# Streaming the columns of a matmul alternately from two halves of its operand

## The chip, the cores and the metric

The kernel runs on one core of one Trainium2 chip. The time is what the device takes for one execution of the program, in microseconds; of several runs the median is given. The profile is that of one further execution, and its own time stands beside the runs below.

## What is computed

Attention in which a query sees only the keys of its own cluster, and then two layers of the form "matmul, activation, matmul" on the 1536 tokens:

```python
scores = np.where(mask, scale * np.matmul(q, k.transpose(0, 1, 3, 2)), -1000000000.0)
attn = softmax(scores)                       # q, k, v: 2 x 8 x 768 x 64
x = heads_side_by_side(np.matmul(attn, v))   # 1536 x 512
h = x @ w_in                                 # 512 -> 2048, layer 1
x = softplus(h) @ w_out                      # 2048 -> 512
h = x @ w_in2                                # the same sizes, layer 2
out = (h * np.clip(h + 3.0, 0.0, 6.0) / 6.0) @ w_out2
```

`mask` is true where the query and the key have the same nearest centroid. The two weights of a layer arrive as float64.

## The kernel before

The attention phase fills the first 268 us or so of the span. It leaves its result transposed in SBUF: `xhi[c]` and `xlo[c]`, four tiles each of 128 features x 1536 tokens. Every float32 operand of the layers is a pair: a rounded part (`hi`, type F32R) and what the rounding left (`lo`). A product is then three matmuls: hi x hi, lo x hi and hi x lo.

The layers run in steps. A step is one layer, one block of 512 tokens (`TB`, three blocks) and one slice f of 128 hidden features (sixteen). For each step:

- `phase_a` (line 172) makes the hidden slice `h` in one PSUM bank, 128 hidden features x 512 tokens: four feature tiles c times three matmuls, twelve in all. The loaded weights are `w[:, c, :]`, a 128x128 piece of w_in; the operand that streams through is `x[c][:, cols]`, 512 tokens in one run.
- `hid_scalar`, `hid_gate`, `hid_hi` and `hid_lo` (lines 865 to 882) read `h` from PSUM and write the activated slice as the pair `ghi`, `glo` in SBUF. In layer 1 ScalarE reads `h` twice (lines 868 and 869) and VectorE makes `glo` (line 882). In layer 2 ScalarE makes `u` from `h` (line 871), VectorE multiplies `u` and `h` (line 875), and ScalarE rounds (line 879).
- `phase_b` (lines 901 and 903) adds the slice's part to four accumulators `y`, one PSUM bank each: again twelve matmuls. In layer 1 (line 901) w_out is loaded and the slice `ghi` or `glo` streams, 512 tokens. In layer 2 (line 903) the slice is loaded and w_out streams, 512 output features, so that the result has tokens as its rows.

After the sixteenth slice of a block `finish_block` reads the four accumulators: in layer 1 into `xhi` and `xlo` (lines 910 and 911), in layer 2 into the tile `o` (lines 918, 919, 924, 926), which SyncE's queue writes to DRAM.

The order is written out by hand. On TensorE `phase_a` of step n is followed by `phase_b` of step n - 2 (`LAG = 2`), so a hidden slice has four groups of twelve matmuls between its making and its use. `h` has four banks, the accumulators one each. The weights are brought from float64 to pairs by ScalarE and VectorE (lines 112 to 147), interleaved with the steps; `convert_abs` (line 112) and `convert_bits` (lines 122 and 126) read one of every two 32-bit words of the loaded weights.

```python
hs[n][:, :TB], w[:, c, :], x[c][:, cols], start=(c == 0 and i == 0), ...
nc.scalar.activation(t["g"], t["h"], AF.Softplus)
nc.tensor.matmul(y[:, :TB], w[:, e, :], x, **fl)
nc.tensor.matmul(y, x[:, e * P:(e + 1) * P], w.rearrange("p c e -> p (c e)"), **fl)
```

Of the kernel before, what the change touches and what calls it, by code (L numbers as in the profile page):

```python
# [12 lines left out]
AF = mybir.ActivationFunctionType  # L13
ALU = mybir.AluOpType
# [8 lines left out]
def cluster_attention_then_two_mlps(  # L23
# [12 lines left out]
    nc = tc.nc  # L36
    P = 128
# [6 lines left out]
    NT, DM = out.shape  # L44
    DFF = w_in1.shape[1]
    NF = DFF // P
    NC = DM // P
# [3 lines left out]
    scale = 1.0 / float(D) ** 0.5  # L51
    assert 2 * D == P and H * C == P and NC == NPAIR and B * S == NT

    def f32(ap):
        return ap.bitcast(F32)
# [20 lines left out]
    xhi = [xpool.tile([P, NT], F32R, name=f"xhi{c}") for c in range(NC)]  # L76
    xlo = [xpool.tile([P, NT], F32R, name=f"xlo{c}") for c in range(NC)]
# [79 lines left out]
    TB = 512  # L157
# [3 lines left out]
    hs = {}  # L161
    last_flip = []

    def phase_a(n, c):
        layer, tb, f = steps[n]
        if c == 0:
            pl, tag = (ps_p, "prep") if n % 4 == 0 else (ps_h[0], "h")
            hs[n] = pl.tile([P, 512], F32, tag=tag, name="h")
        hi_w, lo_w = weights[layer, f, "i"]
        cols = slice(tb * TB, (tb + 1) * TB)  # L170
        for i, (w, x) in enumerate(((hi_w, xhi), (lo_w, xhi), (hi_w, xlo))):
            nc.tensor.matmul(  # L172
                hs[n][:, :TB], w[:, c, :], x[c][:, cols], start=(c == 0 and i == 0), stop=(c == NC - 1 and i == 2)
            )

    def attention():
        with ExitStack() as st, ExitStack() as st_ld, ExitStack() as st_ps:
# [462 lines left out]
            at(87, 6, fetch_w, 0, 6)  # L640
            at(94, 3, open_hidden)
            at(88, 2, phase_a, 0, 0)
            at(90, 1, phase_a, 0, 1)
            at(91, 1, phase_a, 0, 2)
            at(93, 2, phase_a, 0, 3)
            at(94, 3, phase_a, 1, 0)
# [213 lines left out]
    half = const.tile([P, 1], F32, name="half")  # L860
    nc.vector.memset(half, 0.5)

    def hid_scalar(t):

        if t["layer"] == 0:
            nc.scalar.activation(t["g"], t["h"], AF.Softplus)  # L868
            nc.scalar.activation(t["ghi"], t["h"], AF.Softplus)  # L869
        else:  # L870
            nc.scalar.activation(t["u"], t["h"], AF.Relu, bias=half, scale=1.0 / 6.0)  # L871

    def hid_gate(t):
        if t["layer"] == 1:
            nc.vector.scalar_tensor_tensor(t["g"], t["u"], 1.0, t["h"], ALU.min, ALU.mult)  # L875

    def hid_hi(t):
        if t["layer"] == 1:
# [5 lines left out]
    def hidden(layer, h):  # L884
        t = {"h": h, "layer": layer}
        t["ghi"] = tmp.tile([P, TB], F32R, tag="ghi", name="ghi")
        t["glo"] = tmp.tile([P, TB], F32R, tag="glo", name="glo")
        t["g"] = tmp.tile([P, TB], F32, tag="g", name="g")
        if layer == 1:
            t["u"] = tmp.tile([P, TB], F32, tag="u", name="u", bufs=2)  # L890
        return t

    def phase_b(layer, f, g, ys):
        ghi, glo = g["ghi"], g["glo"]
        hi_w, lo_w = weights[layer, f, "o"]
        terms = ((hi_w, ghi), (lo_w, ghi), (hi_w, glo))
        for e, y in enumerate(ys):
            for n, (w, x) in enumerate(terms):
                fl = dict(start=(f == 0 and n == 0), stop=(f == NF - 1 and n == 2))
                if layer == 0:  # L900
                    nc.tensor.matmul(y[:, :TB], w[:, e, :], x, **fl)  # L901
                else:
                    nc.tensor.matmul(y, x[:, e * P:(e + 1) * P], w.rearrange("p c e -> p (c e)"), **fl)  # L903

    def finish_block(layer, tb, ys):
        cols = slice(tb * TB, (tb + 1) * TB)
        if layer == 0:
            for e in range(NC):
                y = ys[e][:, :TB]
                nc.scalar.activation(xhi[e][:, cols], y, AF.Copy)  # L910
                nc.vector.tensor_tensor(xlo[e][:, cols], y, f32(xhi[e][:, cols]), ALU.subtract)
        else:
            for t in range(TB // P):
                o = wpools["val"].tile([P, DM], F32, tag="val", name="o")
                c = tb * (TB // P) + t
                dst = out_v[c // NJ, c % NJ]
                if c == NT // P - 1:
                    nc.scalar.activation(o[:, :DM // 2], ys[t][:, :DM // 2], AF.Copy)
                    nc.vector.tensor_copy(o[:, DM // 2:], ys[t][:, DM // 2:])
                    nc.scalar.dma_start(dst[:, :DM // 2], o[:, :DM // 2])  # L920
                    nc.sync.dma_start(dst[:, DM // 2:], o[:, DM // 2:])
                    continue
                if t % 2:
                    nc.vector.tensor_copy(o, ys[t])
                else:
                    nc.scalar.activation(o, ys[t], AF.Copy)
                nc.sync.dma_start(dst, o)

    LAG = 2
# [8 lines left out]
    with tc.manual_schedule():  # L938
# [11 lines left out]
        for n in range(len(steps) + LAG):  # L950
# [3 lines left out]
            t = None  # L954
            if n < len(steps):
# [3 lines left out]
                t = gs[steps[n]] = hidden(steps[n][0], hs.pop(n)[:, :TB])  # L959
# [9 lines left out]
            if t:  # L969

                with tc.issue_after(last_flip[0].ins):
                    hid_scalar(t)
            do(convert_rest, ci, engine=nc.vector)
            do(convert_abs, ni)
            if t:
                hid_gate(t)
# [6 lines left out]
            if n >= LAG:  # L983
                l, tb, f = s = steps[n - LAG]
                if f == 0:
                    ysd[l, tb] = [
                        ps_y.tile([P, 512], F32, tag=f"y{e}", name=f"y{e}") for e in range(NC)
                    ]
                phase_b(l, f, gs.pop(s), ysd[l, tb])
                if l == 0 and tb == NB - 1:  # L990
                    fetch_w(1, f)
                if f == NF - 1:
                    finish_block(l, tb, ysd.pop((l, tb)))
# [40 lines left out]
```

## Time and profile before

| | us |
|---|---|
| median of three runs | 775.82 |
| the three runs | 774.63, 775.82, 777.75 |
| the profiled execution, its own time | 779.6 |
| its span, first to last instruction | 777.8 |

| engine | busy us | share of the span |
|---|---|---|
| TensorE, matmuls | 761.5 | 98% |
| TensorE, weight loads | 645.0 | 83% |
| VectorE | 457.1 | 59% |
| ScalarE | 409.9 | 53% |
| GpSimd | 150.3 | 19% |

The times of the profile are those of one execution. A matmul's row runs from its start to its modelled end, and the next matmul starts before that end, so rows overlap: how fast matmuls follow each other is read from their starts. "PE" is TensorE's matmuls, "PEld" its weight loads, "DVE" VectorE, "ACT" ScalarE, "POOL" GpSimd, "SP" SyncE. A line number is that of the kernel before.

### The profile page before, as it was taken

How to read it: one execution, taken by the hardware profiler on the slowest of the kernel's cores; microseconds unless marked ns; L12 is line 12 of the kernel's file. 1: busy time of each engine (PE TensorE's matmuls, PEld its weight loads, DVE VectorE, ACT ScalarE, POOL GpSimd, SP SyncE). 2: the span in 40 equal slices, each digit the busy share in tenths (PEclk: the TensorE clock that was granted, in tenths of full speed). 3: DMA queues.
4: the chain of work that ended last, by engine and by line, in shares of the span. 5: the costliest groups of instructions: out<-in, count | busy, mean ns of one | idle time of the engine just before them, and what ended most of it. 6: DMA issues, size and time to landing. Idle time of an engine off the chain costs nothing.

```text
span 777.8 us, 10594 instructions
## 1 busy us (share of the span) xinstructions
PE 761.5 (98%) x3841; PEld 645.0 (83%) x3841; DVE 457.1 (59%) x788; ACT 409.9 (53%) x815; POOL 150.3 (19%) x223
## 2 busy tenths in 40 slices
PE   7989999999999999999999999999999999999998
PEld 6778898899888788888888888888888888888886
DVE  6969889889888999821111276779842322232221
ACT  6869889888998766531121344555532322222222
POOL 3467668767444000000000000000000000000000
PEclk9999999999999999999999999999999999999999
DMA  6645676666463670000000355640000100010001
GB/s 190 178 125 144 172 200 168 157 188 159 113 190 133 223 285 1 1 1 0 1 1 27 109 191 188 201 151 0 1 1 0 55 1 0 1 55 0 1 1 54
DMA packets 40548, 71.32 MB, mean 92 GB/s; under 512 B 4752, under 2 KB 25648, under 8 KB 40496
## 3 DMA queue, kind: packets, MB, share of 16 engines
q1 hardware_dynamic: 40352, 70.52, 30.8%
q8 instruction: 30, 0.49, 0.2%
q14 instruction: 22, 0.18, 0.1%
q10 hardware_dynamic: 144, 0.13, 0.0%
HBM read 46.30 MB, written 3.19 MB: 64 GB/s over the span
## 4 chain that ended last, share of the span: by engine, by line
PE 88%; DVE 3%; ACT 3%; DMA 2%; POOL 2%; issue 1%; POOLq 0%; SPq 0%; ACTq 0%; DVEq 0%
PE h L172 32%; PE y L903 17%; PE y L901 16%; PE t L441 7%; PE pv L456 7%; PE s L411 6%; PE psm L311 2%; DMA q<-in_q 1%; DMA row<-rT 1%; ACT pth L445 1%; DVE nm L419 1%; ACT pr L427 1%; DVE ptl L446 1%; DMA rsb<-row 1%; PE warm L248 0%
## 5 line engine op out<-in xcount | busy, mean ns | idle before, releaser
L172 PE MATMUL h<-xhi,pi 128*128 128x512 f32 x768 | 237.2, 390 | 0.9 <-DVE pi L147 0.8
L172 PEld LDWEIGHTS h<-xhi,pi 128*128 128x128 f32 x768 | 143.7, 188 | 31.0 <-DVE pi L147 1.2
L882 DVE TENSOR_TENSOR glo<-g,ghi 128x512 fp32r<-128x512 f32 x96 | 66.3, 691 | 144.5 <-ACT ghi L869 115.7
L172 PE MATMUL h<-xlo,pi 128*128 128x512 f32 x384 | 149.5, 389 | 0.0
L901 PE MATMUL y<-ghi,po 128*128 128x512 f32 x384 | 118.2, 389 | 0.0
L903 PE MATMUL y<-po,ghi 128*128 128x512 f32 x384 | 118.2, 389 | 0.0
L446 DVE TENSOR_TENSOR ptl<-t,pth 128x384 fp32r<-128x384 f32 x192 | 97.6, 549 | 24.0 <-ACT pth L445 23.0
L875 DVE SCALAR_TENSOR_TENSOR g<-u,h 128x512 f32<-128x512 f32 x48 | 33.0, 687 | 125.1 <-ACT u L871 125.1
L871 ACT ACTIVATE u<-h,half 128x512 f32<-128x512 f32 x48 | 33.0, 687 | 126.1 <-PE h L172 125.8
L411 PE MATMUL s<-K,Q 128*128 128x256 f32 (+1 forms) x384 | 90.2, 356 | 5.6 <-ACT pr L427 3.7
L445 ACT ACTIVATE pth<-t 128x384 fp32r<-128x384 f32 x192 | 85.8, 491 | 15.3 <-PE t L441 14.5
L419 DVE TENSOR_REDUCE nm<-s 128x1 f32<-128x768 f32 x96 | 90.6, 944 | 3.1 <-PE s L411 3.1
L427 ACT ACTIVATE pr<-s,nm 128x768 f32<-128x768 f32 x96 | 86.9, 905 | 3.2 <-DVE nm L419 3.0
L441 PE MATMUL t<-ident,pr 128*128 128x128 f32 x576 | 85.9, 279 | 2.1 <-DVE ptl L446 1.8
L868 ACT ACTIVATE g<-h 128x512 f32<-128x512 f32 x48 | 28.5, 594 | 109.4 <-PE h L172 109.3
L903 PEld LDWEIGHTS y<-po,ghi 128*128 128x128 f32 x384 | 72.1, 188 | 15.0
L172 PEld LDWEIGHTS h<-xlo,pi 128*128 128x128 f32 x384 | 72.1, 188 | 15.0
L901 PEld LDWEIGHTS y<-ghi,po 128*128 128x128 f32 x384 | 72.1, 188 | 15.0
L441 PEld LDWEIGHTS t<-ident,pr 128*128 128x128 f32 x576 | 66.1, 141 | 15.7 <-DVE ptl L446 11.9
L411 PEld LDWEIGHTS s<-K,Q 128*128 128x128 f32 x384 | 66.0, 189 | 15.7 <-ACT pr L427 5.0
L901 PE MATMUL y<-glo,po 128*128 128x512 f32 x192 | 74.7, 389 | 0.0
L903 PE MATMUL y<-po,glo 128*128 128x512 f32 x192 | 74.7, 389 | 0.0
(127 smaller groups left out, 932.5 us busy)
## 6 DMA issues: line engine op xcount, KB each, us to landing
ri<-in_moe_w_in SPq DMA_DIRECT2D x29, 512.0 KB, 4.8
ro<-in_moe_w_out SPq DMA_DIRECT2D x29, 512.0 KB, 8.3
K<-hik SPq DMA_DIRECT2D x31, 192.0 KB, 5.0
Q<-hiq SPq DMA_DIRECT2D x15, 384.0 KB, 3.9
Q<-loq SPq DMA_DIRECT2D x16, 192.0 KB, 5.6
v<-in_v SPq DMA_DIRECT2D x8, 384.0 KB
rsb<-row SPq DMA_DIRECT2D x16, 192.0 KB, 4.1
K<-lok SPq DMA_DIRECT2D x15, 192.0 KB, 4.4
```

The lines of the kernel that those rows point to most:

```text
L172: nc.tensor.matmul(hs[n][:, :TB], w[:, c, :], x[c][:, cols], start=(c == 0 and i == 0), stop=(c == NC - 1 and i == 2))
L411: nc.tensor.matmul(ps[:, n0:n1], Q[i][:, u, j * P:(j + 1) * P], K[i][:, u, n0:n1], start=(u == 0), stop=(u == 1),)
L419: nc.vector.tensor_reduce(nm, st_s[t][:, :S], AX.X, ALU.max, negate=True)
L427: nc.scalar.activation(pr, st_s.pop(t)[:, :S], AF.Exp, bias=st_p[t], accum_out=sums_of[n][:, i, j:j + 1])
L441: nc.tensor.transpose(pt[:, c * P:(c + 1) * P], pr[:, kt * P:(kt + 1) * P], ident)
L445: last_flip[:] = [nc.scalar.activation(dh, src, AF.Copy)]
L446: nc.vector.tensor_tensor(dl, src, f32(dh), ALU.subtract)
L456: nc.tensor.matmul(st_v[h][:, :HALF], vs[:, kt, i, :], st_t[h][u][:, kt, :], start=(kt == 0 and u == 0), stop=(kt == NJ - 1 and u == 1),)
L871: nc.scalar.activation(t["u"], t["h"], AF.Relu, bias=half, scale=1.0 / 6.0)
L882: nc.vector.tensor_tensor(t["glo"], t["g"], f32(t["ghi"]), ALU.subtract)
L901: nc.tensor.matmul(y[:, :TB], w[:, e, :], x, **fl)
L903: nc.tensor.matmul(y, x[:, e * P:(e + 1) * P], w.rearrange("p c e -> p (c e)"), **fl)
```

## The change

Two views of an operand are introduced. `turned` takes 512 columns in the order 0, 256, 1, 257, 2, 258 and so on. The streaming operand of every matmul in both layers is read through it: `x[c][:, cols]` in `phase_a`, the hidden slice in `phase_b` of layer 1, w_out in `phase_b` of layer 2. The matmul's output is written to PSUM as before, in one run, so that the even words of a bank now hold the first 256 columns and the odd words the other 256. `in_order` is the view that undoes it: it reads the even words of a PSUM tile and then the odd ones. Each instruction of ScalarE or VectorE that reads a layer's `h` or `y` reads it through `in_order`; `halved` gives its output the matching shape of two halves without changing the order in memory. The loaded weights, the attention phase, all loads and stores, the number of instructions and their order on every engine are the same.

```diff
+    def turned(ap):
+        return ap.rearrange("p (a b) -> p b a", a=2)
...
         for i, (w, x) in enumerate(((hi_w, xhi), (lo_w, xhi), (hi_w, xlo))):
             nc.tensor.matmul(
-                hs[n][:, :TB], w[:, c, :], x[c][:, cols], start=(c == 0 and i == 0), stop=(c == NC - 1 and i == 2)
+                hs[n][:, :TB], w[:, c, :], turned(x[c][:, cols]), start=(c == 0 and i == 0), stop=(c == NC - 1 and i == 2)
             )
...
+    def in_order(ps):
+        return ps.rearrange("p (b a) -> p a b", a=2)
+
+    def halved(ap):
+        return ap.rearrange("p (a b) -> p a b", a=2)
...
-            nc.scalar.activation(t["g"], t["h"], AF.Softplus)
-            nc.scalar.activation(t["ghi"], t["h"], AF.Softplus)
+            nc.scalar.activation(halved(t["g"]), in_order(t["h"]), AF.Softplus)
+            nc.scalar.activation(halved(t["ghi"]), in_order(t["h"]), AF.Softplus)
         else:
-            nc.scalar.activation(t["u"], t["h"], AF.Relu, bias=half, scale=1.0 / 6.0)
+            nc.scalar.activation(halved(t["u"]), in_order(t["h"]), AF.Relu, bias=half, scale=1.0 / 6.0)
...
-            nc.vector.scalar_tensor_tensor(t["g"], t["u"], 1.0, t["h"], ALU.min, ALU.mult)
+            nc.vector.scalar_tensor_tensor(
+                halved(t["g"]), halved(t["u"]), 1.0, in_order(t["h"]), ALU.min, ALU.mult
+            )
...
                 if layer == 0:
-                    nc.tensor.matmul(y[:, :TB], w[:, e, :], x, **fl)
+                    nc.tensor.matmul(y[:, :TB], w[:, e, :], turned(x), **fl)
                 else:
-                    nc.tensor.matmul(y, x[:, e * P:(e + 1) * P], w.rearrange("p c e -> p (c e)"), **fl)
+                    nc.tensor.matmul(y, x[:, e * P:(e + 1) * P], turned(w.rearrange("p c e -> p (c e)")), **fl)
...
             for e in range(NC):
-                y = ys[e][:, :TB]
-                nc.scalar.activation(xhi[e][:, cols], y, AF.Copy)
-                nc.vector.tensor_tensor(xlo[e][:, cols], y, f32(xhi[e][:, cols]), ALU.subtract)
+                y = in_order(ys[e][:, :TB])
+                hi, lo = halved(xhi[e][:, cols]), halved(xlo[e][:, cols])
+                nc.scalar.activation(hi, y, AF.Copy)
+                nc.vector.tensor_tensor(lo, y, f32(hi), ALU.subtract)
...
                 if c == NT // P - 1:
-                    nc.scalar.activation(o[:, :DM // 2], ys[t][:, :DM // 2], AF.Copy)
-                    nc.vector.tensor_copy(o[:, DM // 2:], ys[t][:, DM // 2:])
+                    y = in_order(ys[t])
+                    nc.scalar.activation(o[:, :DM // 2], y[:, 0], AF.Copy)
+                    nc.vector.tensor_copy(o[:, DM // 2:], y[:, 1])
...
                 if t % 2:
-                    nc.vector.tensor_copy(o, ys[t])
+                    nc.vector.tensor_copy(halved(o), in_order(ys[t]))
                 else:
-                    nc.scalar.activation(o, ys[t], AF.Copy)
+                    nc.scalar.activation(halved(o), in_order(ys[t]), AF.Copy)
```

## Rows read from the trace of the kernel before

**Rows 1.** The page: busy time by engine, and the chain by engine and line.

```profile
PE 761.5 (98%) x3841; PEld 645.0 (83%) x3841; DVE 457.1 (59%) x788; ACT 409.9 (53%) x815; POOL 150.3 (19%) x223
...
PE 88%; DVE 3%; ACT 3%; DMA 2%; POOL 2%; issue 1%; POOLq 0%; SPq 0%; ACTq 0%; DVEq 0%
PE h L172 32%; PE y L903 17%; PE y L901 16%; PE t L441 7%; PE pv L456 7%; PE s L411 6%; PE psm L311 2%; DMA q<-in_q 1%; DMA row<-rT 1%; ACT pth L445 1%; DVE nm L419 1%; ACT pr L427 1%; DVE ptl L446 1%; DMA rsb<-row 1%; PE warm L248 0%
```

**Rows 2.** The chain in order of time, a block's end: start us, us, what.

```profile
341.61 2.72 PE y L901 x12
344.33 2.72 PE h L172 x12
347.05 2.72 PE y L901 x12
...
352.49 2.72 PE y L901 x12
```

**Rows 3.** A stretch: us, PE, PEld, DVE, ACT, POOL busy (x), clock, DMA share, GB/s.

```profile
300.00:400.00 100.00, 100.00 (x443) 82.81 (x442) 38.18 (x65) 33.09 (x62) 0.00 (x0) 1.00 0.00 1
```

**Rows 4.** Groups of matmuls: xcount | busy us, mean ns | idle before.

```profile
L172 PE MATMUL h<-xhi,pi 128*128 128x512 f32 x768 | 237.2, 390 | 0.9 <-DVE pi L147 0.8
L172 PE MATMUL h<-xlo,pi 128*128 128x512 f32 x384 | 149.5, 389 | 0.0
L901 PE MATMUL y<-ghi,po 128*128 128x512 f32 x384 | 118.2, 389 | 0.0
L903 PE MATMUL y<-po,ghi 128*128 128x512 f32 x384 | 118.2, 389 | 0.0
L441 PE MATMUL t<-ident,pr 128*128 128x128 f32 x576 | 85.9, 279 | 2.1 <-DVE ptl L446 1.8
L901 PE MATMUL y<-glo,po 128*128 128x512 f32 x192 | 74.7, 389 | 0.0
L903 PE MATMUL y<-po,glo 128*128 128x512 f32 x192 | 74.7, 389 | 0.0
...
L248 PE MATMUL warm<-ident 128*128 128x128 f32 x15 | 3.5, 425 | 2.1 <-POOL ident masks.py:199 2.1
```

**Rows 5.** The same view, ScalarE and VectorE on 128x512 in SBUF.

```profile
L112 ACT ACTIVATE val<-ri 128x512 f32<-128x512 f32 x32 | 21.5, 672 | 0.0
...
L136 ACT ACTIVATE pi<-val 128x512 fp32r<-128x512 f32 x32 | 20.3, 633 | 50.0 <-DVE val L126 49.9
...
L126 DVE SCALAR_TENSOR_TENSOR val<-ri,val 128x512 uint32<-128x512 uint32 x32 | 22.0, 686 | 0.3
...
L147 DVE TENSOR_TENSOR po<-val,po 128x512 fp32r<-128x512 f32 x30 | 20.6, 685 | 0.2 <-ACT po L136 0.2
```

**Rows 6.** Timeline of TensorE in the attention phase: start us, us, what.

```profile
99.75 0.33 PE L456 MATMUL pv<-pth,vs 128*128 128x384 f32 x1
...
100.27 0.34 PE L456 MATMUL pv<-ptl,vs 128*128 128x384 f32 x1
100.45 0.82 PE L441 MATMUL t<-ident,pr 128*128 128x128 f32 x6
```

**Rows 7.** The same view at the start of the span.

```profile
2.09 3.46 PE L248 MATMUL warm<-ident 128*128 128x128 f32 x15 [2.09 <-POOL ident masks.py:199]
```

**Rows 8.** Timeline of ScalarE and VectorE in one step of layer 1.

```profile
352.53 0.60 ACT L868 ACTIVATE g<-h 128x512 f32<-128x512 f32 x1 [4.35 <-PE h L172]
...
353.65 0.69 DVE L882 TENSOR_TENSOR glo<-g,ghi 128x512 fp32r<-128x512 f32 x1 [4.75 <-ACT ghi L869]
```

**Rows 9.** The same view at a block's end.

```profile
342.62 2.35 ACT L910 ACTIVATE xhi<-y 128x512 fp32r<-128x512 f32 x4
...
343.38 2.48 DVE L911 TENSOR_TENSOR xlo<-y,xhi 128x512 fp32r<-128x512 f32 x4
```

**Rows 10.** The same view at the end of the span.

```profile
774.13 0.38 ACT L918 ACTIVATE o<-y 128x256 f32<-128x256 f32 x1
...
774.55 0.42 DVE L919 COPY o<-y 128x256 f32<-128x256 f32 x1 [1.08 <-ACT o L918]
```

## The prediction

> **What bounds the kernel now.** I read the page's busy line and its chain first [rows 1]. TensorE is busy 761.5 us of the 777.8 us span, and 88% of the chain that ended last is TensorE's own work: 32% in line 172 (the first matmul of a layer), 17% in line 903 and 16% in line 901 (the second). The reader should see that the two layers alone are 65% of the time and that almost none of it is a wait. A busy TensorE is not yet one at its peak, since a matmul's row (389 ns) overlaps the next, so the rate comes from the chain in order of time [rows 2]: the twelve matmuls of one group take 2.72 us, one group follows the other without a gap, and so a 128x512 matmul takes 2.72 / 12 = 226.7 ns. [...]
>
> How many matmuls the change touches comes from the groups of instructions [rows 4]: 768 + 384 of line 172, 384 + 192 of line 901, 384 + 192 of line 903, in all 2304. At 226.7 ns these are 522 us, two thirds of the kernel.
>
> **The change part by part.** No instruction is added, removed or moved: every engine's queue, DMAs included, keeps its order. What differs is the order of the addresses inside instructions.
>
> *The moving operand.* Each of the 2304 matmuls now reads column 0, 256, 1, 257 and so on, two places 1 KB apart by turns, and writes PSUM in one run as before. The trace of before has no matmul that reads so, thus the price is bounded. From below: nothing, if TensorE takes two alternating runs as easily as one. A first step up is ScalarE, the nearest row of a read that is not word after word [rows 5]: line 112 reads every second word of SBUF and takes 672 ns, line 136 reads 512 words in one run and takes 633 ns, so 39 ns a 512. VectorE's line 126, which reads every second word too, takes 686 against 685 ns of line 147, so nothing. From above: TensorE itself has rows where a column takes longer. The f32 transposes of line 441 are six in 0.82 us; less one's own 0.28 us that is 0.54 / 5 = 108 ns for 128 columns, 0.84 ns a column, about two cycles [rows 4, 6]. [...]
>
> I take two cycles a column. [...] That ScalarE already pays 39 ns on every second word points the same way, and two cycles is the nearest slower rate at which the trace shows TensorE in the steady state. A matmul then takes 2 x 213.3 + 13.4 = 440 ns, 213.3 more. The sum: 2304 x 213.3 ns = 491.4 us, all on the path, since the chain is these matmuls without a gap.
>
> The row on ScalarE says that leaving out words costs an engine a little (39 ns). [...]
>
> *The reads out of PSUM.* Lines 868, 869, 871, 875, 910, 911, 924 and 926 now read every second word, first the even ones, then the odd. Below: 0 (VectorE's line 126). Above: twice their 0.59 to 0.69 us. I take 39 ns on ScalarE and 0 on VectorE [rows 5], and it is covered: ScalarE sits idle 4.35 us before line 868, and glo of the step whose h ends at about 352.5 us is written by 354.34 us; the matmuls that read it start four groups later, at 352.49 + 4 x 2.72 = 363.4 us, 9 us after it [rows 2, 8]. At the end of a token block the four accumulators are read from 342.62 to 345.86 us, and the next group that writes them starts at 347.05 us, and reaches the fourth of them nine matmuls later, at 349.09 us [rows 2, 9]. If that cover were gone (reads twice as long), VectorE would end at about 349.4 us, some 0.3 us late, at five block ends 1.5 us. Open to view are only the last two copies, 0.38 and 0.42 us [rows 10]: between 0 and 0.8 us. The SBUF writes stay in runs and cost nothing more.
>
> The attention phase, up to 268 us, is not touched but for the 24 matmuls of line 172 that already count.
>
> Sum against the profiled execution: span 777.8 + 491.4 = 1269 us; its own time 779.6 gives 1271 us. That execution is 3.8 us above the median of the runs, 775.82, so the forecast for a median is 775.8 + 491.4 = **1267 us**. A difference of 0.5%, 3.9 us, is about what a measurement of this kernel can tell from none.
>
> **The rivals.**
>
> *The alternation is free* (0.24): TensorE holds both runs at once, or the pattern does not reach its reader as written. For it speaks that the columns of each run still follow word after word, and that VectorE's row shows no toll. Against it, that TensorE draws words three times as fast as that row. What is left is the tail, under 0.8 us: 776 us. [...]
>
> *A partial toll* (0.16): something between nothing and a cycle a column, as line 112 pays. At 39 ns a matmul 775.8 + 90 = 866 us. For it, that this is the only measured toll of a broken run in this kernel; against it, that it belongs to another engine.
>
> *Four cycles a column* (0.15): if a column waits for a fetch that served four. At the 1.69 ns of line 248 a matmul is 864 ns, 637 more, 1468 us in all: 2244 us. Against it, that this rate stands only at the start of the trace.
>
> [...]
>
> **How the numbers follow.** Two cycles a column has 0.40; with it the range is 1225 to 1290 us (0.80 to 0.85 ns a column, and the PSUM reads at their upper bound). With the free case (775), the partial toll and this, 0.80 is held by 775 to 1290 us; four cycles and faster are left out. Slower by over 0.5%: 0.40 + 0.16 + 0.15 = 0.71; within 0.5%: 0.24; faster: 0.05. The wide range is that of the free case and the slow one together; the likeliest case's own is the narrow one.
>
> **What would show it.** Right: in the chain a group of twelve takes 5.28 us in place of 2.72, lines 172, 901 and 903 alike, the granted clock stays 1.00, the attention phase ends where it did, and ScalarE's idle time before line 868 grows by over 5 us. [...] Wrong: groups still at 2.72 us (free), near 3.2 us (partial) or 10.4 us (four cycles); a difference between line 172 or 901 and line 903, whose moving operand is a weight; or TensorE idle before line 901 or 903 with VectorE or ScalarE as the releaser, which would put the cost into the PSUM reads.

## The result, and the profile after

The changed kernel takes 756.61 us (median of four runs, 756.49 to 756.96) against 776.72 us of the kernel before (four runs, 774.63 to 777.75): a ratio of the means of 0.9745, with a 95% interval of 0.9722 to 0.9768. It is 20.1 us faster, where the forecast was 1267 us and the range began at 775.

The page of the changed kernel, its busy line and its chain, which answer to [rows 1]:

```profile
PE 737.6 (98%) x3841; PEld 645.2 (86%) x3841; DVE 472.4 (63%) x788; ACT 418.4 (55%) x815; POOL 151.5 (20%) x223
...
PE 80%; DVE 9%; issue 3%; ACT 3%; DMA 3%; SPq 1%; POOL 1%; POOLq 0%; DVEq 0%; ACTq 0%
PE h L177 28%; PE y L918 16%; PE y L916 12%; PE t L446 7%; PE s L416 7%; PE pv L461 7%; DVE val L122 3%; PE psm L316 2%; DVE val L126 2%; DVE val L120 1%; DMA ro<-in_moe_w_out 1%; DVE glo L897 1%; DVE nm L424 1%; ACT pth L450 1%; DVE ptl L4
```

TensorE still sets most of the chain, but VectorE's part has risen from 3% to 9%, in lines 120 to 126, the conversion of the weights. (Lines 172, 901 and 903 of the kernel before are 177, 916 and 918 here.)

The chain of the changed kernel in order of time, the same place as [rows 2]:

```profile
338.69 2.59 PE y L916 x12
341.28 2.59 PE h L177 x12
343.87 2.59 PE y L916 x12
```

A group of twelve takes 2.59 us where it took 2.72, in both lines. Over the 2304 matmuls the start-to-start time fell from 226.7 to 2.59 / 12 = 215.8 ns, 10.9 ns each, at a granted clock of 1.00 in both kernels (330 to 400 us, stretches below). The sum, 2304 x 10.9 ns = 25.1 us, is 5 us more than the result.

Where the 5 us went is in the stretches, nearly all of which belong to the layers: in the trace of the kernel before, lines 172 and 901 follow each other from 258.7 us on, earlier than the 268 us that the text ahead of the prediction gives for the end of the attention phase. Stretches of the kernel before (columns as in [rows 3]: length, busy time and instructions of TensorE, weight loads, VectorE, ScalarE, GpSimd, granted clock, DMA):

```profile
255.00:270.00 15.00, 14.19 (x64) 11.68 (x65) 14.63 (x27) 11.24 (x21) 0.00 (x0) 1.00 0.65 228
270.00:300.00 30.00, 30.00 (x134) 24.82 (x134) 29.62 (x54) 18.98 (x36) 0.00 (x0) 1.00 0.57 215
300.00:330.00 30.00, 30.00 (x134) 24.85 (x133) 26.79 (x48) 16.80 (x32) 0.00 (x0) 1.00 0.00 1
330.00:400.00 70.00, 70.00 (x311) 57.96 (x310) 11.39 (x17) 16.29 (x30) 0.00 (x0) 1.00 0.00 0
```

The same stretches of the changed kernel:

```profile
255.00:270.00 15.00, 13.29 (x59) 10.77 (x59) 14.86 (x25) 9.35 (x18) 0.00 (x0) 1.00 0.98 340
270.00:300.00 30.00, 29.15 (x131) 23.95 (x130) 29.62 (x50) 18.87 (x33) 0.00 (x0) 1.00 0.42 159
300.00:330.00 30.00, 29.16 (x131) 23.95 (x130) 28.48 (x47) 18.38 (x32) 0.00 (x0) 1.00 0.00 1
330.00:400.00 70.00, 70.00 (x326) 61.31 (x325) 11.57 (x18) 16.18 (x30) 0.00 (x0) 1.00 0.00 1
```

From 330 us on TensorE issues 326 matmuls in 70 us where it issued 311. From 270 to 330 us it issues 131 + 131, six fewer than before, and is no longer busy all the time. VectorE is busy 29.62 of 30 us in both kernels, but gets 50 instructions done for 54. The groups of instructions tell which became slower. First the reads out of PSUM of the kernel before:

```profile
L868 ACT ACTIVATE g<-h 128x512 f32<-128x512 f32 x48 | 28.5, 594 | 109.4 <-PE h L172 109.3
L875 DVE SCALAR_TENSOR_TENSOR g<-u,h 128x512 f32<-128x512 f32 x48 | 33.0, 687 | 125.1 <-ACT u L871 125.1
```

ScalarE of the changed kernel, the same read out of PSUM and the answers to [rows 5]:

```profile
L881 ACT ACTIVATE g<-h 128x512 f32<-128x512 f32 x48 | 28.4, 591 | 91.8 <-PE h L177 91.8
...
L112 ACT ACTIVATE val<-ro 128x512 f32<-128x512 f32 x32 | 27.3, 852 | 1.0 <-POOL pi L147 1.0
L112 ACT ACTIVATE val<-ri 128x512 f32<-128x512 f32 x32 | 25.9, 809 | 0.0
```

VectorE, the same:

```profile
L888 DVE SCALAR_TENSOR_TENSOR g<-u,h 128x512 f32<-128x512 f32 x48 | 32.9, 686 | 107.3 <-ACT u L884 107.3
L126 DVE SCALAR_TENSOR_TENSOR val<-ri,val 128x512 uint32<-128x512 uint32 x32 | 26.5, 829 | 0.3
```

The reads of the raw weights, every second word of SBUF, rose from 672 to 809 ns (tile `ri`) and from 670 to 852 ns (tile `ro`) on ScalarE and from 686 to 829 ns on VectorE, though the change does not touch them. The reads out of PSUM by every second word cost nothing (591 ns for 594, 686 for 687), and line 136, which reads SBUF in one run, takes 632 ns for 633. The timeline shows the consequence. TensorE of the changed kernel in one step:

```profile
291.46 0.38 PE L177 MATMUL h<-xhi,pi 128*128 128x512 f32 x1
292.02 0.48 PE L177 MATMUL h<-xhi,pi 128*128 128x512 f32 x1 [0.18 <-DVE pi L147]
```

VectorE in the same step:

```profile
290.51 0.85 DVE L122 SCALAR_TENSOR_TENSOR val<-ro,val 128x512 uint32<-128x512 uint32 x1
291.30 0.67 DVE L147 TENSOR_TENSOR pi<-val,pi 128x512 fp32r<-128x512 f32 x1
```

A second matmul of line 177 starts 0.56 us after the first in place of 0.216: it waits for the rest part of the weight that line 147 writes at 291.97 us, behind a read of 0.85 us.

### The profile page after: what moved, and what is told of

It reads as the page before. It is cut to its first block, busy times and chain, and to the rows that moved or that the text cites. A ratio compares the mean times of both kernels' runs of the same rounds, so it can differ in the third digit from the quotient of the medians.

```text
span 754.3 us, 10558 instructions
## 1 busy us (share of the span) xinstructions
PE 737.6 (98%) x3841; PEld 645.2 (86%) x3841; DVE 472.4 (63%) x788; ACT 418.4 (55%) x815; POOL 151.5 (20%) x223
## 4 chain that ended last, share of the span: by engine, by line
PE 80%; DVE 9%; issue 3%; ACT 3%; DMA 3%; SPq 1%; POOL 1%; POOLq 0%; DVEq 0%; ACTq 0%
PE h L177 28%; PE y L918 16%; PE y L916 12%; PE t L446 7%; PE s L416 7%; PE pv L461 7%; DVE val L122 3%; PE psm L316 2%; DVE val L126 2%; DVE val L120 1%; DMA ro<-in_moe_w_out 1%; DVE glo L897 1%; DVE nm L424 1%; ACT pth L450 1%; DVE ptl L451 1%
## 5 line engine op out<-in xcount | busy, mean ns | idle before, releaser
L177 PE MATMUL h<-xhi,pi 128*128 128x512 f32 x768 | 232.1, 381 | 3.5 <-DVE pi L147 2.8
L177 PE MATMUL h<-xlo,pi 128*128 128x512 f32 x384 | 145.5, 379 | 0.0
L916 PE MATMUL y<-ghi,po 128*128 128x512 f32 x384 | 114.3, 379 | 0.0
L918 PE MATMUL y<-po,ghi 128*128 128x512 f32 x384 | 114.2, 379 | 0.0
L916 PE MATMUL y<-glo,po 128*128 128x512 f32 x192 | 72.8, 379 | 0.0
L918 PE MATMUL y<-po,glo 128*128 128x512 f32 x192 | 72.8, 379 | 0.0
```

The lines of the kernel that those rows point to most:

```text
L177: nc.tensor.matmul(hs[n][:, :TB], w[:, c, :], turned(x[c][:, cols]), start=(c == 0 and i == 0), stop=(c == NC - 1 and i == 2))
L916: nc.tensor.matmul(y[:, :TB], w[:, e, :], turned(x), **fl)
L918: nc.tensor.matmul(y, x[:, e * P:(e + 1) * P], turned(w.rearrange("p c e -> p (c e)")), **fl)
```

## The experiments

Kernels that run together are compared with runs of the kernel before on the same chip. In all but two of them (called e9 and e10 below) the instructions that read PSUM go over their words in one run, as the texts say, so that the stream of the matmuls (in e8 the loaded weights) is the only thing that differs. The number to read is the time of a group of twelve in the chain at 400 us, away from the conversion of the weights. Apart from e9 and e10 each kernel ran once; the kernel before alone lies between 774.41 and 779.71 us in these runs, so a few microseconds between two of these times say nothing.

The theories on the stream, by the letters used here: any break between neighbouring columns helps (N), two places far apart do (F), the mere form of the pattern does (D), an unbroken stream pays a fixed cost per matmul (M), the cost comes from the weight load and the stream meeting (C), the reader holds the pieces it reads from by turns (H).

**The stream alone.**

```diff
     def in_order(ps):
-        return ps.rearrange("p (b a) -> p a b", a=2)
+        return ps.rearrange("p (a b) -> p a b", a=2)
```

> The matmuls stream alternately from the two halves as in the change, but every read out of PSUM goes over its words in one run again; the columns of each 512 therefore stay in the streamed order and the numbers of the output are permuted. If the gain sits in the stream alone (theory S), a group of twelve matmuls stays at 2.59 us, as in the change, and the time is that of the change, 756.6 us, within 1 us. If the reads by every second word cost or gave something (theory R), ScalarE's and VectorE's reads of h and y change by more than 20 ns and the time by more than 2 us. The slower reads of the raw weights seen in the change (809 to 852 ns on ScalarE for 672, 826 on VectorE for 690) stay under S and vanish under R.

Measured: 759.49 us beside 779.32 of the kernel before, 19.8 us less; a group at 2.59 us, line 112 at 812 and 853 ns. The time is 2.9 us above that of the change, but its kernel before is 2.6 us above as well. Theory S holds: the stream alone is changed here, so gain and slow reads both come from it.

**Hop inside eight bytes; runs of four; runs of 64.**

```diff
     def turned(ap):
-        return ap.rearrange("p (a b) -> p b a", a=2)
+        return ap.rearrange("p (k a b) -> p k b a", a=2, b=2)    # e2: 0, 2, 1, 3
+        return ap.rearrange("p (a b r) -> p b a r", a=2, r=4)    # e3: runs of four
+        return ap.rearrange("p (a b r) -> p b a r", a=2, r=64)   # e4: runs of 64
```

> The stream takes the columns in the order 0, 2, 1, 3, 4, 6, 5, 7: no two consecutive addresses follow each other upwards except once in four, but the stream stays in one place; PSUM is read in one run, so the output is permuted. If any break of the run by one word is what helps (theory N, neighbours), a group of twelve is at 2.59 us or most of the way to it (under 2.65). If the gain needs two places far apart (theory F), it stays at 2.72 us. If it is only that the pattern has more than one dimension (theory D), 2.59 us.

> The stream alternates between the two halves, but in runs of four columns; PSUM is read in one run, so the output is permuted. Theory N: three of four steps are to the neighbour again, so 2.69 us or more. Theory F, two places far apart in turn: 2.59 us still, or between. Theory D, the form of the pattern: 2.59 us. The slow reads of the raw weights by ScalarE and VectorE (over 800 ns in the change) should fall back towards 672 and 690 ns if they come from a hop at every column.

> The stream alternates between the two halves in runs of 64 columns, eight hops in a matmul, with a pattern of as many dimensions as the run of four; PSUM is read in one run, so the output is permuted. Theory D, the form of the pattern alone: 2.59 us. Theories N and F: 2.72 us, that of the kernel before.

Measured, the chain in order of time; the hop inside eight bytes (775.46 us, before 779.32):

```profile
402.39 2.72 PE y L916 x12
```

Runs of four (829.12 us):

```profile
400.37 3.00 PE y L916 x12
```

Runs of 64 (778.89 us):

```profile
400.39 2.72 PE y L916 x12
```

A pattern of two or three dimensions is not what helps (theory D falls with e2 and e4), and neither is any break between neighbours (theory N falls with e2). Runs of four are dearer than an unbroken stream.

The slow reads of the raw weights should have fallen back with runs of four if a hop at every column made them; they did not. ScalarE in that run:

```profile
L112 ACT ACTIVATE val<-ri 128x512 f32<-128x512 f32 x32 | 27.3, 854 | 0.0
L136 ACT ACTIVATE pi<-val 128x512 fp32r<-128x512 f32 x32 | 21.4, 667 | 51.4 <-DVE val L126 51.4
```

Here even line 136, which reads in one run, is slower (667 ns for 633). With runs of 64 line 112 is back at 671 ns.

**Two places 16 or 128 bytes apart; pairs; the weights' addresses.**

```diff
+        return ap.rearrange("p (k a b) -> p k b a", a=2, b=4)    # e5: 16 bytes
+        return ap.rearrange("p (k a b) -> p k b a", a=2, b=32)   # e6: 128 bytes
+        return ap.rearrange("p (a b r) -> p b a r", a=2, r=2)    # e7: pairs, 1 KB
+        w.rearrange("p c e -> p (c e)")[:, c::NC]                # e8: loaded weights
```

> The stream alternates between two places 16 bytes apart (columns 0, 4, 1, 5, 2, 6, 3, 7, then the next eight); PSUM is read in one run, so the output is permuted. Theory M (a stream that is fetched in larger pieces pays some 11 ns once per matmul; one that leaves the piece at every column is fetched word by word at full rate and does not pay): if the piece is 16 bytes, a group of twelve is at 2.59 us here; if it is larger, 2.72 us, as with the hop inside 8 or 16 bytes. Theory F (two places far apart): 2.72 us.

> The stream alternates between two places 128 bytes apart, 64 columns at a time; PSUM is read in one run, so the output is permuted. Theory M with a piece of at most 64 bytes: 2.59 us, and ScalarE's and VectorE's reads of the raw weights rise to over 800 ns as in the change. Theory F with a need for 1 KB: 2.72 us and the reads stay near 672 and 690 ns. Were the gain and the slow reads one thing, they come and go together in this run and in that with 16 bytes.

> The stream alternates between the two halves in pairs of columns; PSUM is read in one run, so the output is permuted. Runs of one gave 2.59 us a group, runs of four 3.00 us, runs of 64 2.72 us. If the cost of a run of four is that of a fetch thrown away half used, pairs lie above 2.72 us too, up to twice (5.3 us) if each pair is one fetch. If words are fetched one by one as soon as the pattern hops often, pairs are at 2.59 us like runs of one.

> The stream is that of the kernel before, in one run, and PSUM is read in one run; the 128 loaded weight columns are every fourth of the 512 instead of 128 in a row, so the output is another permutation of the features and not the reference's. [...]

The kernel before took 775.94 us here. 16 bytes: 755.09 us.

```profile
404.68 2.59 PE y L916 x12
```

128 bytes: 752.82 us.

```profile
402.40 2.59 PE y L916 x12
```

Pairs: 1022.0 us.

```profile
404.28 4.00 PE y L916 x12
```

So a hop of 16 bytes gives the whole gain and a hop of 8 bytes none; theory F falls. The gain and the slow reads are two things. Line 112 with 16 bytes, with 128 bytes and with pairs:

```profile
L112 ACT ACTIVATE val<-ri 128x512 f32<-128x512 f32 x32 | 21.5, 672 | 0.0
L112 ACT ACTIVATE val<-ri 128x512 f32<-128x512 f32 x32 | 22.0, 687 | 0.0
L112 ACT ACTIVATE val<-ri 128x512 f32<-128x512 f32 x32 | 22.1, 691 | 0.1
```

With 1 KB and a hop at every column it takes 809 to 853 ns. The pairs hop by 1 KB too, and their reads stay near 690 ns, so the distance alone does not make the reads slow. Pairs cost 333 ns a matmul, 0.65 ns a column, 1.5 times what single columns take: two columns at each place are dearer than one.

The kernel with other weight addresses was to try theory C: if load and stream meet, a group leaves 2.72 us and the loads leave 188 ns. It took 794.7 us. Its stretch shows why that does not decide the theory:

```profile
400.00:450.00 50.00, 50.00 (x214) 50.00 (x214) 8.63 (x13) 11.95 (x22) 0.00 (x0) 1.00 0.17 53
```

The weight loads went from 188 to 310 ns and fill 50 of 50 us: they leave TensorE no room and may set the pace themselves (a group at 2.82 us). The run is inconclusive on whether loads and stream meet.

**The columns put back in order, and the attention phase.** e9 is as e6, with ghi, glo and the results written in the columns' own order; e10 does the same for the scores, the similarities and the weighted values too.

```diff
-            nc.scalar.activation(t["ghi"], t["g"], AF.Copy)
+            nc.scalar.activation(halved(t["ghi"]), in_order(t["g"]), AF.Copy)
...
-                        st_v[h][:, :HALF], vs[:, kt, i, :], st_t[h][u][:, kt, :],
+                        st_v[h][:, :HALF], vs[:, kt, i, :], turned(st_t[h][u][:, kt, :]),
```

> The stream alternates between two places 128 bytes apart, in blocks of 64 columns, and the columns are put back in order where ghi, glo and the results are written, so nothing is left out. If the 6 us that the change lost in the stretch from 255 to 340 us come from the slow reads of the raw weights next to a stream with 1 KB between its two places, this kernel keeps 2.59 us a group and reads the raw weights in under 700 ns, TensorE's waits in that stretch fall below 2 us, and the time is 752 to 754 us against 756.6 for the change. If the conversion falls behind simply because TensorE is faster, the waits stay near 6 us and the time near 756 us.

> As the kernel with 128 bytes between the two places, and the matmuls of the attention phase stream alternately too (512 and 256 columns for the scores, 384 for the weighted values and the similarities), put back in order by the instructions that read PSUM. If the cost of an unbroken stream is fixed per matmul (theory M), the spacing of the 384-column matmuls falls from 174 to about 163 ns, as much as that of the 512-column ones; if it is a sixteenth of the columns, to about 166 ns. The attention phase is not bound by TensorE alone: 384 x 11 ns of weighted values and as much of the scores are 8 us, of which I expect 2 to 8 us in the time, 745 to 751 us; with the phase bound by ScalarE and VectorE, nothing, 753 us.

Measured: 751.06 us in the layers alone, a ratio of 0.9682 (0.9651 to 0.9712); 746.23 us with the attention phase, 0.9621 (0.9585 to 0.9657); the kernel before 774.89 us in these runs. Stretches of the first of the two:

```profile
255.00:270.00 15.00, 13.63 (x64) 11.57 (x63) 14.63 (x28) 9.79 (x19) 0.00 (x0) 1.00 1.00 341
270.00:300.00 30.00, 30.00 (x141) 26.27 (x140) 29.59 (x54) 18.91 (x36) 0.00 (x0) 1.00 0.42 159
300.00:330.00 30.00, 30.00 (x141) 26.27 (x140) 23.53 (x42) 16.66 (x31) 0.00 (x0) 1.00 0.00 1
```

TensorE is busy all the time again: 64 + 141 + 141 = 346 matmuls where the change issued 321, that is 25 x 0.216 = 5.4 us, about the part of the gain that was missing. Line 112 takes 688 and 692 ns here, and the time is just under the 752 to 754 us expected. So it was the slow reads, and not the faster TensorE as such, that held the change back. Timeline of TensorE in the attention phase of the second, as [rows 6]:

```profile
99.96 0.33 PE L469 MATMUL pv<-pth,vs 128*128 128x384 f32 x1
...
100.45 0.33 PE L469 MATMUL pv<-ptl,vs 128*128 128x384 f32 x1
100.61 0.82 PE L454 MATMUL t<-ident,pr 128*128 128x128 f32 x6
```

The spacing is 0.65 / 4 = 163 ns where it was 175: 12 ns less, where the layers' 512 columns saved 11, as a fixed cost per matmul (theory M) would have it. The time fell by 4.8 us. But the scores in the same traces do not fit a fixed cost. Of the kernel before, the second matmul of 512 columns with the first of 256, and then the two of 256:

```profile
99.28 0.51 PE L411 MATMUL s<-K,Q 128*128 128x512 f32 x2
99.51 0.40 PE L411 MATMUL s<-K,Q 128*128 128x256 f32 x2
```

The same of e10:

```profile
99.52 0.49 PE L424 MATMUL s<-K,Q 128*128 128x512 f32 x2
99.73 0.39 PE L424 MATMUL s<-K,Q 128*128 128x256 f32 x2
```

By the starts in the trace, which the rows round, the next start came 233 ns after the matmul of 512 columns and comes 215 ns after it now (medians of all 96 such: 232 and 216, 16 ns less); for the two of 256 columns it is 237 ns and 221 ns, 8 ns less each. So the saving is 8, 12 and 16 ns for 256, 384 and 512 columns here, and 11 for 512 in the layers. Neither a fixed cost per matmul nor one per column gives all four; what sets it stays open.

**Every fourth column; 512 bytes.**

```diff
+        return ap.rearrange("p (a b) -> p b a", b=4)             # e11: 0, 4, 8, ...
+        return ap.rearrange("p (k a b) -> p k b a", a=2, b=128)  # e12: 512 bytes
```

> The stream takes every fourth column, 0, 4, 8 to 508, then 1, 5 and so on: each column lies 16 bytes behind the last, and none of the last hundred lies within the same 16 bytes; PSUM is read in one run, so the output is permuted. If the alternation is quick because TensorE's reader holds two pieces of 16 bytes and serves the turns from them (theory H), this stream has no such luck and a group takes well over 2.72 us, up to 10 us. If words that do not follow each other are fetched one by one at a word per cycle wherever they lie (theory M), 2.59 us.

> The stream alternates between two places 512 bytes apart, in blocks of 256 columns; PSUM is read in one run, so the output is permuted. A group takes 2.59 us. For the raw weights' reads: near 690 ns as with 128 bytes, or over 800 ns as with 1 KB; if it is 1 KB itself, or a multiple that the two reads share, that makes the engines meet, this run lies with the low ones; if the cost grows with the distance, in between.

Measured: every fourth column, 1313.14 us.

```profile
405.04 5.54 PE y L916 x12
```

That is 461 ns a matmul, 0.90 ns a column, 2.1 times the 216 ns of two places by turns. A reader that fetches single words at full rate wherever they lie (that part of theory M) is ruled out; one that serves the turns from pieces of 16 bytes it still holds (theory H) fits this run, but not the pairs, which take turns between two places as well and cost 333 ns. With 512 bytes between the places: 759.5 us, a group at 2.59 us, and the raw weights' reads are slow again:

```profile
L112 ACT ACTIVATE val<-ro 128x512 f32<-128x512 f32 x32 | 27.5, 861 | 3.5 <-POOL pi L147 3.5
```

So 1 KB itself is not special; with a hop at every column the border lies between 128 and 512 bytes.

**Four places; unbroken and alternating matmuls mixed.**

```diff
+        return ap.rearrange("p (k a b) -> p k b a", a=4, b=4)    # e13
...
+                hs[n][:, :TB], w[:, c, :], x[c][:, cols] if i == 1 else turned(x[c][:, cols]), ...   # e15
```

> The stream goes round four places 16 bytes apart (columns 0, 4, 8, 12, 1, 5, 9, 13 and so on, sixteen columns a round of four); PSUM is read in one run, so the output is permuted. If the reader holds the pieces of two places only (theory H2), every read meets a piece that is not held and a group takes about 12 x 461 = 5.53 us, as with every fourth column. If it holds four (theory H4), 2.59 us. Something between would say that the toll depends on how soon a piece comes again.

> Of the three matmuls of each product the first and third stream alternately (128 bytes apart), the second in one run; sums of differently ordered columns are added, so the output means nothing. If the 11 ns belong to the unbroken matmul itself, 768 of the 2304 pay it: the spacing from an unbroken matmul to the next start is about 227 ns and all others 216 ns, or, if the cost lies ahead of its own start, from the matmul before it; a group takes 2.59 + 4 x 0.011 = 2.63 us. If it belongs to a change of pattern or to both neighbours, 2.68 us or more; if one alternating matmul in between clears it, 2.59 us.

Measured: four places 874.38 us, 269 ns a matmul:

```profile
404.52 3.22 PE h L177 x12
```

Neither the 5.53 us of two held pieces nor the 2.59 us of four: the toll lies between, so whether pieces are held, and how many, is not settled. The mixed kernel took 767.39 us, the kernel before 776.11. Its timeline of TensorE, where a row of two is an alternating and then an unbroken matmul:

```profile
400.67 0.61 PE L177 MATMUL h<-xhi,pi 128*128 128x512 f32 x2
401.12 0.38 PE L177 MATMUL h<-xlo,pi 128*128 128x512 f32 x1
401.34 0.61 PE L916 MATMUL y<-ghi,po 128*128 128x512 f32 x2
401.79 0.38 PE L916 MATMUL y<-glo,po 128*128 128x512 f32 x1
```

A pair takes 0.45 us and a single alternating matmul 0.22. By the starts in the trace the next matmul comes 215 or 216 ns after an alternating one, also where the next one is unbroken, and 235 to 237 ns after an unbroken one. So the extra time stands behind the unbroken matmul. It is 20 ns here rather than 11, and the group takes 2.67 us, nearer to the 2.68 expected of a change of pattern than to the 2.63 of a cost of the unbroken matmul alone. Whether the change back to alternation adds a part is not settled.

## Why the prediction was wrong

*What bounds the kernel* was right: TensorE's spacing, 226.7 ns, 2304 times, nearly all of it on the path. So was what followed from it, that a change of spacing goes into the time almost in full (23.8 us of 25.1 in e9). Of line 172, 49 matmuls and not 24 start before 268 us, which changes nothing in the sum.

*The moving operand* is the step that failed: "I take two cycles a column." Measured was 215.8 ns a matmul where 440 were forecast: the term of +213.3 ns a matmul came out as -10.9. No run shows the 213.3 and the 13.4 ns that the 440 are put together from, nor how long a cycle is; the traces show starts 226.7 ns apart with the unbroken stream and 215.8 ns apart with the change, at a granted clock of 1.00 in both. Single columns from two places by turns thus take less than the unbroken stream. Other orders do cost: every fourth column takes 461 ns, close to the 440 I had priced, and pairs from the same two halves 333. That the price nearly fits another pattern is luck. The rows of ScalarE (39 ns) and of line 441 (0.84 ns a column) spoke of other things; no row showed an alternation on TensorE, and a cost for it should not have been made the likeliest on them alone. The dearest price, the 1.69 ns of line 248, is (3.46 - 0.43) / 14 = 216 ns for 128 columns [rows 4, 7]; the dearest order tried took 0.90 ns a column.

*Faster* had a chance of 0.05 and was left out of the range. No row of the kernel before shows how much of the 226.7 ns another order could win back; the runs showed 10.9 ns in the layers, and not why.

*The free case* had its low end at 775 us, so the range took in no gain at all.

*The reads out of PSUM* were right in the time: I took 39 ns on ScalarE and nothing on VectorE, both under cover; measured was nothing on either (591 ns for 594, 686 for 687).

*VectorE and ScalarE* have room by the stretch of [rows 3], 300 to 400 us: right for 330 to 400 us, wrong for 270 to 330 us, where VectorE was busy 29.62 and then 26.79 of 30 us before the change, and where TensorE now waits. The mean of 300 to 400 us hid a stretch with little room. There the faster stream took 5 us of its own gain back, by a way I had not thought of: the stream of one engine slowing the reads of two others. With the stream alone changed, 672 and 670 ns became 812 and 853.

## What to carry to other kernels

If TensorE sets the pace with f32 operands that stream in one run (226.7 ns for 512 columns here), try a stream that alternates column by column between two places 16 to 128 bytes apart (215.8 ns here), and let the engine that reads PSUM put the order back, which cost nothing on ScalarE and VectorE here (591 ns for 594, 686 for 687). Then look at every stretch in which another engine has little room (VectorE 29.62 and 26.79 of 30 us here): that is where the gain stopped, and where the stream's effect on other engines' reads showed. An access pattern without a row of its own is better measured than priced by analogy: single columns, pairs and runs of four from the same two halves took 216, 333 and 250 ns.

## What the runs showed of the hardware

- An unbroken f32 stream costs TensorE time that an alternating one does not pay: 11 ns a matmul of 512 columns in the layers, 20 between alternating ones, and 8, 12 and 16 ns for 256, 384 and 512 columns in the attention phase. Why, and what sets the amount, was not found. A hop of 8 bytes and runs of 64 columns do not remove it (a group at 2.72 us in both).
- The time of a matmul of 512 columns depends on their order: two places 16 bytes to 1 KB apart by turns 216 ns, four places 269, every fourth column 461; with two places 1 KB apart, runs of four 250 and pairs 333. The first three rise with how late a piece of 16 bytes is read again; pairs and runs of four do not fit that, and no theory tried here gives all five.
- A stream that hops at every column between two places 512 bytes or 1 KB apart slows other engines' reads of every second word (ScalarE 807 to 861 ns in place of 670 to 672, VectorE 789 to 830 in place of 684 to 713) and leaves their reads in one run as they were (632 for 633); with 16 bytes it does not (672), with 128 hardly (687). At 1 KB, runs of four slow them too, and the reads in one run with them (667 for 633); pairs hardly (691), runs of 64 not (671). How the stream slows them was not tried.
